# Attention and routed experts on one core: GpSimd's subtractions in four parts, and ScalarE in written order from step 117

## Chip, cores, metric

The kernel runs on one core of a Trainium2 chip. The metric is the device time of one launch in microseconds (us), lower is better. TensorE (PE) multiplies matrices, VectorE (DVE) and GpSimd (POOL) work elementwise, ScalarE (ACT) applies functions and copies, SyncE (SP) issues most of the DMAs. Each engine takes its instructions in the order in which they stand in its own queue, and waits for semaphores of the others.

## What is computed

Attention with rotary embedding over 4 batches, 8 heads, 576 positions and 64 dimensions, and behind it a mixture of 8 experts. A token takes the expert of its largest logit, or, where its local gate is at least one half, the expert of the token before it. Cut to what matters:

```python
scores = (rotate(q) @ rotate(k).T) / sqrt(64)
attn = softmax(scores)
x = (attn @ v) as rows of 512
logits = x @ w_gate; local = sigmoid(x @ w_local)
e[s] = argmax(logits[s]) if s == 0 or local[s] < 0.5 else e[s - 1]
p = softmax(logits[s])
out[s] = p[e] * (relu(x[s] @ w1[e]) @ w2[e])
```

## The kernel before

**Steps of the attention.** Two heads make a pair, so there are 16 pairs, and each has nine tiles of 128 queries: 144 steps g = 0 to 143 (line 1269 on). Step g does the following. DVE takes the minimum of the score tile (`mn`, line 278; the queries are negated). PE makes the scores of step g + 1 (`s`, line 273; two buffers of PSUM, so tile g + 1 needs the exponential of step g - 1 to have read its buffer). ACT takes the exponential (`e`, or `et` for the ninth tile; line 295). PE turns the tile of step g - 2 (`tm`, line 331, and `tk` or `tt` for what is left over), and PE multiplies by the values with a lag of eleven steps (`pv`, line 370).

**The high and low parts.** Matrices are multiplied as a high part and a rest. For a turned tile ACT casts the high part from PSUM (`pth`, line 309) and DVE subtracts it for the rest (`ptl`, line 313). For the steps' tiles in `ON_POOL` (125, 129, 130, 132, 134) `split_by_pool` is used in place of it: ACT copies the tile into SBUF (`stage`, line 304), GpSimd casts it (line 305) and GpSimd subtracts (line 306). The turned tiles, the products with v, the gate products `gx` and the routing's small products share four PSUM buffers. One is free again when its last reader is done.

**Gates and rows.** For a pair two places back, `gates` corrects the sums of the exponentials (ACT, lines 437 and 440; DVE's reciprocal, line 443), PE makes `gx` (line 456), and DVE or GpSimd scale it to logits `gm` (line 469) and to rows `xrow` (line 470), which go to DRAM.

**Routing.** When twelve pairs have their gates, at step 126, the routing of the first three batches is put into `todo`, one part of it for each step in the order of the string `ORDER`. It is a chain of small operations, mostly on DVE: maximum `mx`, difference `d`, exponential `ex` on ACT (line 531), code `c`, `f`, `key`, a scan over the tokens (line 564), the expert `e`, its one-hot `cnt` (line 581), a copy of it by ACT (`oha`, line 582), the running counts `cox`, the sum `se` (ACT adds 1e-9 on line 603), the product `d` with the one-hot on GpSimd (line 609), the probability `p` (lines 612 and 615), ranks (lines 632 to 647; fifteen compares on GpSimd on line 645) and the slots of the expert tiles (lines 682 to 709). Behind it GpSimd splits the first expert's weights (lines 894 and 895) and gathers rows (`x`, line 955). From step 143 on a written list (`DRAIN`) ends the attention. Then come the expert tiles: `tx` turns gathered rows (line 966), and the two products `h` and `o` follow (lines 980 and 1023).

**What sets the order.** Up to step 116 (`GM` is 117) every engine keeps the order in which the code is written. From step 117 to 143 the code runs under `tc.manual_schedule(engines=MAN0)`, and `MAN0` holds PE alone: a scheduler with due times of its own orders ACT, DVE, GpSimd and SP there. The scheduler can bring an operation forward as far as its inputs allow, also into the steps before 117. `late` is a list of work that each step runs behind its exponential.

```python
with tc.manual_schedule(engines=None if g < GM else MAN0):
    ...
    softmax_exp(g, mn)
    ...
    for f in late[:]:
        f()
        late.remove(f)
```

## Time and profile before

| | us |
|---|---|
| median of 3 runs | 538.23 (537.24 to 538.36) |
| profiled execution, its own time | 539.23 |
| profiled execution, span of its instructions | 537.5 |
| PE busy | 516.4 (96%) |
| DVE busy | 381.2 (71%) |
| ACT busy | 345.4 (64%) |
| POOL busy | 344.2 (64%) |

The profile is one execution. Busy shares are averages over stages with different limits: the steps of the attention up to about 285 us, then the expert tiles. Times in the rows below count from the first instruction. A figure in square brackets behind a row is the time for which that engine stood idle before it, and what ended the wait.

### The profile page before, as it was taken

Reading aid. Unit: us, or ns where it says so; the run is one execution under the profiler, and the core shown is the slowest. Engines: PE = TensorE matmul, PEld = TensorE weight load, DVE = VectorE, ACT = ScalarE, POOL = GpSimd, SP = SyncE. Lnnn points to the kernel's source line nnn. Section 1 sums busy time; section 2 is a strip of 40 time slices with the busy share of each in tenths; the row PEclk is TensorE's granted clock in tenths of the full one; section 3 lists DMA queues with packets and bytes.
Section 4 is the critical chain, followed back from the end, with each engine's and each line's share of the span. In section 5 each row is a group of like instructions: output and inputs, shape, how many; then the busy total and the mean of one; then the engine's idle time right before and its main releaser. Section 6 shows DMA issues by size and latency. Waiting matters only on the chain.

```text
span 537.5 us, 10798 instructions
## 1 busy us (share of the span) xinstructions
PE 516.4 (96%) x3273; PEld 459.1 (85%) x3273; DVE 381.2 (71%) x690; ACT 345.4 (64%) x766; POOL 344.2 (64%) x275
## 2 busy tenths in 40 slices
PE   7989999999999999999889999999999999999992
PEld 4889999999999999998889788887888888888881
DVE  6999999999999999999998746447421745421740
ACT  3988999999999999987667424352433344523440
POOL 4999999999999999694698202355512554411331
PEclk9999999999999999999999999999999999999998
DMA  8658788988889878865167214553537586637440
GB/s 277 277 133 223 223 221 230 239 187 213 222 224 241 213 188 217 239 157 134 21 221 212 70 29 168 183 211 107 187 101 234 142 331 167 187 99 234 107 150 25
DMA packets 65481, 97.33 MB, mean 181 GB/s; under 512 B 28353, under 2 KB 39105, under 8 KB 65282
## 3 DMA queue, kind: packets, MB, share of 16 engines
q1 hardware_dynamic: 61938, 86.45, 57.1%
q0 software_dynamic: 3040, 9.71, 5.8%
q8 instruction: 28, 0.46, 0.4%
q14 instruction: 43, 0.35, 0.2%
q10 hardware_dynamic: 432, 0.36, 0.2%
HBM read 76.95 MB, written 12.86 MB: 167 GB/s over the span
## 4 chain that ended last, share of the span: by engine, by line
PE 79%; DVE 10%; issue 3%; ACT 3%; POOL 2%; DMA 1%; ACTq 0%; POOLq 0%; DVEq 0%
PE h L980 18%; PE o L1023 17%; PE pv L370 14%; PE s L273 13%; PE tm L331 9%; PE gx L456 3%; DVE mn L278 3%; DVE ptl L313 2%; PE th L1014 2%; PE tx L966 1%; PE tk L341 1%; ACT e L295 1%; DVE w L925 1%; DMA turn<-in_turn_dram 1%; ACT w L922 1%
## 5 line engine op out<-in xcount | busy, mean ns | idle before, releaser
L1023 PE MATMUL o<-w,hs 128*128 128x512 f32 x456 | 113.0, 398 | 0.0
L278 DVE TENSOR_REDUCE mn<-s 128x1 f32<-128x576 f32 x144 | 107.1, 744 | 2.3 <-PE s L273 0.9
L295 ACT ACTIVATE e<-s,mn 128x576 f32<-128x576 f32 x128 | 95.5, 746 | 18.5 <-DVE mn L278 16.1
L980 PE MATMUL h<-w,xs 128*128 128x512 f32 x444 | 106.1, 392 | 0.8 <-DVE xs L313 0.5
L313 DVE TENSOR_TENSOR ptl<-tm,pth 128x512 fp32r<-128x512 f32 x139 | 95.5, 688 | 11.6 <-ACT pth L309 8.9
L1029 POOL DMA_INDIRECT out_dram<-os,sidx x19 | 23.2, 1223 | 124.1 <-ACTq L931 82.8
L273 PE MATMUL s<-m,qst 128*128 128x288 f32 x512 | 96.8, 311 | 4.7 <-ACT e L295 2.7
L980 PEld LDWEIGHTS h<-w,xs 128*128 128x128 f32 x444 | 82.6, 188 | 19.0 <-DVE w L925 1.1
L1023 PEld LDWEIGHTS o<-w,hs 128*128 128x128 f32 x456 | 83.1, 188 | 17.0 <-DVE hs L313 0.4
L309 ACT CAST pth<-tm 128x512 fp32r<-128x512 f32 x139 | 80.7, 581 | 6.8 <-PE tm L331 6.1
L273 PEld LDWEIGHTS s<-m,qst 128*128 128x128 f32 x512 | 74.0, 188 | 10.2 <-ACT e L295 5.4
L370 PE MATMUL pv<-pth,v 128*128 128x288 f32 x256 | 76.6, 314 | 0.5 <-DVE ex_row L723 0.4
L331 PE MATMUL tm<-wid,e 128*128 128x128 f32 x512 | 77.0, 272 | 0.0
L370 PE MATMUL pv<-ptl,v 128*128 128x288 f32 x256 | 76.3, 314 | 0.0
L200 POOL TENSOR_TENSOR stage<-stage 128x1152 f32<-128x1152 f32 x26 | 69.4, 2668 | 0.3 <-DMA stage<-in_qk_dram 0.3
L331 PEld LDWEIGHTS tm<-wid,e 128*128 128x128 f32 x512 | 62.0, 140 | 0.9 <-DVE ptl L313 0.3
L925 DVE TENSOR_TENSOR w<-stage,w 128x1024 fp32r<-128x1024 f32 x37 | 50.7, 1406 | 14.5 <-ACT w L922 9.4
L370 PEld LDWEIGHTS pv<-pth,v 128*128 128x128 f32 x256 | 48.3, 189 | 2.0 <-issue 0.6
L370 PEld LDWEIGHTS pv<-ptl,v 128*128 128x128 f32 x256 | 48.3, 189 | 0.0
L313 DVE TENSOR_TENSOR xs<-tx,xs 128x512 fp32r<-128x512 f32 x19 | 13.1, 689 | 44.3 <-ACTq L931 34.5
L201 POOL TENSOR_TENSOR stage<-stage 128x576 f32<-128x576 f32 x26 | 37.1, 1426 | 2.0
L313 DVE TENSOR_TENSOR hs<-th,hs 128x512 fp32r<-128x512 f32 x26 | 17.5, 688 | 27.9 <-ACTq L931 16.4
(202 smaller groups left out, 824.0 us busy)
## 6 DMA issues: line engine op xcount, KB each, us to landing
stage<-in_wts_dram SPq DMA_DIRECT2D x84, 512.0 KB
stage<-in_qk_dram SPq DMA_DIRECT2D x26, 576.0 KB
qst<-xq SPq DMA_DIRECT2D x56, 128.0 KB
stage<-in_v_dram SPq DMA_DIRECT2D x16, 320.0 KB
m<-xq SPq DMA_DIRECT2D x14, 288.0 KB
m<-xk SPq DMA_DIRECT2D x14, 288.0 KB
m<-xq SPq DMA_DIRECT2D x14, 256.0 KB
m<-xk SPq DMA_DIRECT2D x14, 256.0 KB
```

The source lines that it names most:

```text
L200: engine.tensor_tensor(x, x, tab[:, 2 * f:2 * f + 2], op=ALU.mult)
L201: engine.tensor_tensor(rr[:, f], x[:, 0], x[:, 1], op=ALU.add)
L273: pe.matmul(st[:, h, lo:hi], lhs, keys[:, k0:k0 + hi - lo], start=(n == 0), stop=(n == len(parts_) - 1))
L278: dve.tensor_reduce(mn, s_t[g][:, :, 0:HALF], axis=AX.XY, op=ALU.min)
L295: act.activation(dst.rearrange("p (h s) -> p h s", h=2), s_t.pop(g)[:, :, 0:HALF], AF.Exp, bias=mn, scale=-1.0, accum_out=sums[:, col:col ...
L309: act.copy(hi, src)
L313: dve.tensor_tensor(lo, src, hi.bitcast(F32), op=ALU.subtract)
L331: pe.transpose(ps[:, k], src[:, k * P:(k + 1) * P], ident)
L370: pe.matmul(pv_t[p, u], lhs.rearrange("p c d -> p (c d)"), rhs, start=(n == 0), stop=(n == 9))
L925: (pool if k in on_pool else dve).tensor_tensor(lo, src, hi.bitcast(F32), op=ALU.subtract)
L980: pe.matmul(ps[:, c], xs_t[t][:, x, k], w[y][:, c * 512:(c + 1) * 512], start=(k == 0 and n == 0), stop=(k == 3 and n == 2))
L1023: pe.matmul(ps, hs_t[t][:, x, k], w[y][:, (k % 2) * 512:(k % 2 + 1) * 512], start=(k == 0 and n == 0), stop=(k == 7 and n == 2))
```

## The change

There are two edits. `split_by_pool` subtracts in four instructions, one for each 128 columns, where there was one for all 512. `MAN0` takes in ACT, so that from step 117 ACT keeps the written order too; three operations of the first routing on ACT (`ex`, `oha` and the addition to `se`) are put into `late` and run behind the exponential of the next step. DVE, GpSimd and SP are still ordered by the scheduler there. Its answers differ where ACT's order differs.

```diff
-MAN0 = {PE_}
+MAN0 = {PE_, mybir.EngineType.Activation}
...
         pool.tensor_scalar(hi, x, 1.0, 1.0, op0=ALU.mult, op1=ALU.mult)
-        pool.tensor_tensor(lo, x, hi.bitcast(F32), op=ALU.subtract)
+        for k in range(4):
+            pool.tensor_tensor(lo[:, k], x[:, k], hi[:, k].bitcast(F32), op=ALU.subtract)
...
+        def on_act(f):
+            f() if final else late.append(f)
+
...
-            act.activation(ex, d, AF.Exp)
+            on_act(lambda: act.activation(ex, d, AF.Exp))
...
-            act.copy(oh, cnt[:, :, 1:n + 1].rearrange("p e j -> p j e"))
+            on_act(lambda: act.copy(oh, cnt[:, :, 1:n + 1].rearrange("p e j -> p j e")))
...
-            act.add(se, se, 1e-9)
+            on_act(lambda: act.add(se, se, 1e-9))
...
+        assert not late
```

Line numbers of the changed kernel are one higher from the new loop on, four higher from `route` on and five higher in the last part. In the rows below, the number behind a name's first underscore is its pair or a count, and for `tm`, `tk`, `s` and `mn` the step; the last number is a buffer's.

ScalarE from step 125 to step 127, before:

```order
L295 ACTIVATE e_13_3_4164,sum_3_3441<-s_125_4159,mn_125_4187 128x576
L440 ACTIVATE sum_3_3441<-sum_3_3441 128x10
L309 CAST pth_13_3994<-tm_123_4197 128x4x128
L309 CAST pth_13_3994<-tm_124_4216 128x4x128
L295 ACTIVATE et_14_4214,sum_3_3441<-s_126_4189,mn_126_4207 128x576
L531 ACTIVATE ex_5_4233<-d_4_4231 128x120
L295 ACTIVATE e_14_0_4251,sum_3_3441<-s_127_4209,mn_127_4244 128x576
```

The same place after:

```order
L295 ACTIVATE e_13_3_4164,sum_3_3441<-s_125_4159,mn_125_4187 128x576
L310 CAST pth_13_3994<-tm_123_4197 128x4x128
L295 ACTIVATE et_14_4214,sum_3_3441<-s_126_4189,mn_126_4207 128x576
L310 CAST pth_13_3994<-tm_124_4216 128x4x128
L295 ACTIVATE e_14_0_4250,sum_3_3441<-s_127_4209,mn_127_4243 128x576
L535 ACTIVATE ex_5_4233<-d_4_4231 128x120
```

The exponential of step 126 now stands ahead of the cast of tile 124, and the routing's `ex` behind the exponential of step 127. The addition to the sums is gone from here: those of three pairs, which the scheduler had brought forward, now stand at steps 121, 133 and 139.

ScalarE at steps 131 and 132, before:

```order
L304 COPY stage_94<-tm_129_4399 128x512
L295 ACTIVATE e_14_2_4397,sum_3_3441<-s_131_4365,mn_131_4390 128x576
L380 COPY tmp_13_4348<-pv_13_1_4378 64x288
L295 ACTIVATE e_14_2_4397,sum_3_3441<-s_132_4392,mn_132_4431 128x576
L582 CAST oha_107<-cnt_11_4422 128x120
```

The same place after:

```order
L295 ACTIVATE e_14_2_4400,sum_3_3441<-s_131_4368,mn_131_4393 128x576
L304 COPY stage_94<-tm_129_4402 128x512
L381 COPY tmp_13_4351<-pv_13_1_4381 64x288
L295 ACTIVATE e_14_2_4400,sum_3_3441<-s_132_4395,mn_132_4436 128x576
L586 CAST oha_107<-cnt_11_4428 128x120
```

The copy of tile 129, on which GpSimd waits, has gone behind the exponential of step 131.

VectorE around the minimum of step 124, before:

```order
L278 TENSOR_REDUCE mn_124_4157<-s_124_4122 128x1
L313 TENSOR_TENSOR ptl_13_3995<-tm_121_4128,pth_13_3994 128x4x128
L313 TENSOR_TENSOR pkl_13_3997<-tk_121_4135,pkh_13_3996 128x256
L469 TENSOR_TENSOR gm_2_3315<-gx_11_3_4146,sum_2_2278 128x2x18
L470 TENSOR_TENSOR xrow_11_3_4149<-gx_11_3_4146,sum_2_2278 128x256
L278 TENSOR_REDUCE mn_125_4187<-s_125_4159 128x1
```

The same place after:

```order
L314 TENSOR_TENSOR ptl_13_3995<-tm_121_4128,pth_13_3994 128x4x128
L314 TENSOR_TENSOR pkl_13_3997<-tk_121_4135,pkh_13_3996 128x256
L470 TENSOR_TENSOR gm_2_3315<-gx_11_3_4146,sum_2_2278 128x2x18
L471 TENSOR_TENSOR xrow_11_3_4149<-gx_11_3_4146,sum_2_2278 128x256
L278 TENSOR_REDUCE mn_124_4157<-s_124_4122 128x1
L278 TENSOR_REDUCE mn_125_4187<-s_125_4159 128x1
```

The minimum of step 124 has gone behind four operations. The minimum of step 142 goes behind the same four of tile 139 and `gx_13_3`.

## Rows read from the trace of the kernel before

**Rows 1.** The page's forty slices of the span, TensorE's busy share in tenths.

```profile
PE   7989999999999999999889999999999999999992
```

**Rows 2.** Busy time by engine in stretches of 10 us: stretch, length, busy (instructions) per engine.

```profile
260.00:270.00 10.00, 8.46 (x63) 7.72 (x63) 9.94 (x31) 6.95 (x18) 6.80 (x12) 1.00 0.24 32
270.00:280.00 10.00, 9.04 (x67) 8.13 (x66) 9.78 (x22) 6.61 (x16) 9.86 (x15) 1.00 0.73 250
```

**Rows 3.** Timeline of TensorE: start, duration, instruction, idle before and releaser.

```profile
244.62 0.80 PE L273 MATMUL s<-m,qst 128*128 128x288 f32 x4 [0.75 <-ACT et L295]
...
255.50 0.79 PE L273 MATMUL s<-m,qst 128*128 128x288 f32 x4 [0.64 <-ACT e L295]
...
261.87 1.01 PE L456 MATMUL gx<-wid,xt 128*128 128x146 f32 x6 [0.59 <-DVE ptl L313]
...
266.68 0.44 PE L341 MATMUL tk<-wid,e 128*128 128x128 f32 x2 [0.54 <-DVE ptl L313]
...
278.26 0.44 PE L341 MATMUL tk<-wid,e 128*128 128x128 f32 x2 [0.59 <-DVE ptl L313]
```

**Rows 4.** Timeline of VectorE, five operations of the routing.

```profile
255.36 1.70 DVE L581 TENSOR_TENSOR cnt<-cst,e 128x120 bf16<-128x120 f32 x1
...
259.02 1.20 DVE L615 TENSOR_TENSOR p<-p,se 128x15 f32<-128x15 f32 x1
...
264.23 0.99 DVE L647 SCALAR_TENSOR_TENSOR tcode<-e,lb 128x15 f32<-128x15 int32 x1
...
268.42 0.39 DVE L765 TENSOR_SCALAR wgt<-take 128x8 f32<-128x8 f32 x1
...
276.24 1.36 DVE L686 TENSOR_TENSOR ex<-c,cst 128x180 bf16<-128x180 bf16 x1
```

**Rows 5.** Timeline of GpSimd over the same time.

```profile
255.23 1.29 POOL L306 TENSOR_TENSOR ptl<-stage,pth 128x512 fp32r<-128x512 f32 x1
...
257.61 0.63 POOL L609 TENSOR_TENSOR d<-ex,oha 128x120 f32<-128x120 f32 x1 [1.10 <-ACT oha L582]
...
258.92 1.27 POOL L306 TENSOR_TENSOR ptl<-stage,pth 128x512 fp32r<-128x512 f32 x1
...
265.47 8.77 POOL L645 TENSOR_SCALAR ohr<-cst,lc 128x128 bf16<-128x128 bf16 x15
...
276.12 1.28 POOL L306 TENSOR_TENSOR ptl<-stage,pth 128x512 fp32r<-128x512 f32 x1
```

**Rows 6.** Two lines that run in both routings: shortest, median, longest in ns.

```profile
L581 DVE TENSOR_TENSOR cnt<-cst,e x2: 336/1019/1702, 255.4 to 312.9; 128x120 bf16<-128x120 f32 x1, 128x40 bf16<-128x40 f32 x1
...
L647 DVE SCALAR_TENSOR_TENSOR tcode<-e,lb x2: 156/575/994, 264.2 to 321.3; 128x15 f32<-128x15 int32 x1, 128x5 f32<-128x5 int32 x1
```

**Rows 7.** Timeline of GpSimd: a smaller operation on two inputs.

```profile
240.42 0.35 POOL L502 TENSOR_TENSOR gm<-gm 128x90 f32<-128x90 f32 x1
```

**Rows 8.** Timeline of VectorE around step 124.

```profile
237.91 0.75 DVE L278 TENSOR_REDUCE mn<-s 128x1 f32<-128x576 f32 x1
...
239.61 0.41 DVE L470 TENSOR_TENSOR xrow<-gx,sum 128x256 f32<-128x256 f32 x1
```

**Rows 9.** Timeline of ScalarE at steps 124, 126 and 131.

```profile
238.76 0.74 ACT L295 ACTIVATE e<-s,mn 128x576 f32<-128x576 f32 x1 [0.36 <-DVE mn L278]
...
243.24 0.59 ACT L309 CAST pth<-tm 128x512 fp32r<-128x512 f32 x1 [0.60 <-PE tm L331]
...
253.85 0.59 ACT L304 COPY stage<-tm 128x512 f32<-128x512 f32 x1 [1.42 <-PE tm L331]
```

**Rows 10.** Timeline where the attention ends: TensorE, GpSimd's first gather, TensorE.

```profile
285.76 0.98 PE L456 MATMUL gx<-wid,xt 128*128 128x146 f32 x6 [0.24 <-DVE ihi L700]
...
286.12 1.28 POOL L955 DMA_INDIRECT x<-rows_d,gidx  x1 [0.16 <-issue]
...
292.39 0.60 PE L966 MATMUL tx<-wid,x 128*128 128x128 f32 x4
```

**Rows 11.** The tile x between 285.5 and 287 us: the first gather's landing.

```profile
DMA to landing us min/median/max: 3.7/3.7/3.7
```

## The prediction

> **What bounds the kernel now.** I read the page's slices first: TensorE (PE) is at 9 tenths or more in nearly all of them, and the dip between 255 and 282 us is the one inside the span [rows 1]. That is steps 131 to 143, the routing of the first three batches beside the last attention tiles. By stretch, VectorE (DVE) is busy 9.94 and 9.78 of 10 us there while PE is busy 8.46 and 9.04, so PE stands idle 1.54 + 0.96 = 2.50 us in these 20 us [rows 2]. DVE sets the pace. PE's own waits name it: two are for an exponential (0.75 and 0.64 us), three for a subtraction of DVE's (0.59, 0.54 and 0.59 us) that frees a PSUM buffer [rows 3]. Before and behind this stretch PE is full, so a microsecond won here should arrive at the end, and one lost too.
>
> **Why DVE is slow there.** Four of its routing operations take 1.70, 1.20, 0.99 and 1.36 us [rows 4], far above their size. The line that takes 0.99 us with 15 elements takes 0.156 us with 5 in the other routing, and the one with 1.70 us for 120 elements takes 0.336 us for 40 [rows 6]. Three of the four end with a subtraction of GpSimd's: the probability runs from 259.02 to 260.22, and GpSimd's subtraction from 258.92 to 260.19; the operation from 276.24 ends at 277.60, 0.20 us behind GpSimd's 277.40; `cnt` ends 0.54 us behind 256.52, which is about its own time [rows 4, 5]. So a DVE operation of this kind stands until GpSimd's instruction is over. Minima and subtractions from PSUM beside them keep their usual time. During the fifteen compares of GpSimd, 8.77 us without a gap, a DVE operation of 8 elements takes 0.39 us [rows 4, 5]: it gets in between two of them.
>
> **The subtraction in four.** GpSimd's operation on 90 columns takes 0.35 us and on 512 columns 1.28 [rows 5, 7], a slope of 0.93 / 422 = 2.2 ns a column. A part of 128 is then 0.35 + 38 x 2.2 ns = 0.43 us (an estimate), four are 1.73, and each of the five subtractions costs GpSimd 0.45 us more. The upper bound is a compare of 128 columns, 8.77 / 15 = 0.58, so 2.34 and 1.06 us more; the lower is no cost at all, 1.28. I take 0.45, the row of the same operation. A DVE operation caught behind it now waits at most 0.43 us (0.58), on average half of that, in place of up to 1.28.
>
> The rows show only DVE standing. The Trainium skill, "SBUF — State Buffer", section "Who interferes with whom", says that the port pair which the two share is an exclusive lock for a whole instruction, and that the one that issues second blocks, whichever it is. By that, DVE can now also get in front of three more parts and hold up GpSimd; no row here shows GpSimd held. Each such case would cost GpSimd a DVE operation of about 0.2 us, and the sum below would come out 0.2 us worse.
>
> **The four blocked operations, one by one.** (a) `cnt` at step 132 and (b) the probability at step 133: their excess is 1.16 and about 1.03 us. But ACT's written order takes much of it back. The copy of tile 129 ran at 253.85, in an idle stretch of ACT's, ahead of the exponential of step 131 [rows 9]. Now it stands behind that exponential, whose buffer PE waits for until 255.50 [rows 3], so it starts at about 255.45, 1.6 us later. GpSimd then casts until 256.8 and subtracts until 258.55, and the product `d` that stands behind it starts at 258.6 where it started at 257.61 [rows 5]. It ends at 259.2. DVE, in order, has finished `cnt` early (255.9, since GpSimd is idle) and all behind it by 257.5, and then stands until 259.2 for `d`. The probability runs into the next cast of GpSimd and ends near 260.1, against 260.22. Gain here: 0.1, so I write 0. With parts of 0.58 us it is a loss of 0.5.
>
> (c) The line with 0.99 us at 264.23: it now waits 0.2 us for a part and takes about 0.16. Against it stand ACT's correction of the sums of pair 12 (now at step 133, 0.4 us before the copy of tile 132) and DVE's reciprocal of 0.13, both moved here from where PE was full. DVE is then 0.3 us earlier (between 0 and 0.5), and of PE's 0.54 us at 266.68 [rows 3] 0.3 go. (d) The line with 1.36 us at 276.24 becomes 0.3 to 0.7: only one part of tile 134's subtraction stands ahead of GpSimd's next work. The subtraction behind it comes 0.7 us or more earlier, and the whole 0.59 us at 278.26 [rows 3] goes. I take 0.59.
>
> **ACT's written order at step 126.** Before, the exponential of step 126 stood behind a cast for which ACT idled 0.60 us at 243.24 [rows 9], and PE waited 0.75 us for it at 244.62 [rows 3]. It now stands ahead. The new times in this paragraph are estimates: every operation keeps its duration and starts when its inputs and its engine are there. The scheduler has answered on DVE: the minimum of step 124, at 237.91 before, stands behind the row product, which ended at 239.61 + 0.41 = 240.02 [rows 8]. Without the minimum in front, these products end at 239.55. The minimum then runs to 240.2, and the exponential of step 124 starts at 240.2 instead of 238.76 [rows 9]. PE needs its buffer for the scores of step 126, and those of step 127 need the next exponential: PE is 0.45 us late there, then 0.83 (scores of 127 at 242.8). Behind the next minimum (242.65 to 243.35) the exponential of step 126 runs from 243.5 to 244.15, and PE's five products with v are over at 244.6. So PE is at 244.6 in both: the 0.75 us wait is gone, and as much has been spent ahead of it. Sum: 0 (between -0.7 and +0.8). Up to step 130 ACT and DVE then stand as before.
>
> **The end of the stretch.** The minimum of step 142 goes behind four operations in the same way. By its inputs, exponential 142 starts at about 280.4 and the one of step 143 at 282.1, 0.4 us earlier than now, although PE is 0.9 earlier. PE's wait at 285.76 for DVE [rows 10] grows from 0.24 to about 0.5. Given back: 0.3 us.
>
> **GpSimd's chain and its cover.** From the cast of tile 132 to the first gather GpSimd has no gap. The two subtractions inside add 0.9 us and the later start 0.2, so the gather goes from 286.12 to 287.2 and lands 3.7 us behind that [rows 10, 11], at 290.9. PE needs it at 292.39 [rows 10], or 291.8 after a gain of 0.6. The cover is 0.9 us. With parts of 0.58 us the gather is 1.2 us later still, and the missing 0.3 us would be paid in full. SP's queue keeps its order; the loads that wait for GpSimd's weight splits come a microsecond later and are for the second expert tile.
>
> **Sum.** 0 (step 126) + 0 (a, b) + 0.3 (c) + 0.59 (d) - 0.3 (end) = 0.6 us less. Against the profiled execution's own 539.23 that is 538.6; this execution is 1.0 above the median of the runs, 538.23, and from that it is **537.6**. A measurement of this kernel can tell about 0.2% from no change, that is 1.08 us, so the forecast is "the same".
>
> **Rivals.** *DVE's time arrives whole.* If the parts are cheap, or `d` doesn't hold DVE, then four operations lose 4.1 us of excess less a part each (4 x 0.43), 2.4 us, and PE's idle 2.50 us in the stretch [rows 2] fall to about 0.4. That is 2.1 less: 536.1. For it: DVE is the engine that is full. Against: ACT puts GpSimd later just where two of the four are. *The minima late.* The exponentials of steps 124 and 142 stand behind row products, and PE doesn't recover what it loses: 0.83 at step 127, 0.7 at the end, 0.5 at step 133 for `d`, against 0.9 won at (c) and (d). That is 1.1 more: 539.4. It decides from the point at which exponential 126 ends behind 244.4. For it: DVE and ACT had no slack at 238 to 244 beyond what I counted, 0.36 us before exponential 124 [rows 9]. Against: the exponential of step 126 no longer waits for a cast. *The port isn't given up between parts.* Then DVE stands 1.7 us instead of 1.28, (c) and (d) are gone, and the result is 0.3 more: 538.5. Against it are the fifteen compares [rows 4, 5], between which DVE did get in.
>
> **How the numbers follow.** Forecast 0.42, DVE's time whole 0.30, minima late 0.18, port kept 0.10. Below 537.15 lie the second and a small part of the first: faster 0.36. Above 539.3 lies the third: slower 0.18. The rest, 0.46, is the same. The forecast's own range is 537.0 to 538.5. To leave out 2 in 10, the range runs from a little below 536.1 to a little above 539.4.
>
> **What would show it.** Right: the line of `cnt` at 0.5 us and that of 276.24 below 0.8; DVE idle 1 us or more before the sum of `p`, waiting for GpSimd's `d`; no wait of PE at the scores of step 128; idle time of ACT for the minimum of step 124 above 1 us; the wait for a subtraction at tile 139's `tk` gone; the first gather near 287. Wrong: PE's idle time between 260 and 280 below 1 us (the second case), or above 3 us (the third); four parts in more than 2.1 us; a wait of PE at the first `tx`.

## The result, and the profile after

The changed kernel takes 541.96 us (median of 6 runs, 541.10 to 544.24) against 538.22 (6 runs): a ratio of **1.0074, 95% interval 1.0056 to 1.0091**. It is slower, by 3.7 us. The forecast was 537.6, the range ended a little above 539.4, and the case "slower" had 0.18. The profiled execution has a span of 539.6 us and takes 541.53.

The stretches of 10 us, as in [rows 2] (length, then busy time and instructions of PE, PEld, DVE, ACT, POOL, granted clock, DMA):

```profile
240.00:250.00 10.00, 8.12 (x61) 7.51 (x60) 9.55 (x19) 8.23 (x22) 4.86 (x7) 1.00 0.60 142
250.00:260.00 10.00, 9.29 (x73) 8.37 (x72) 8.30 (x17) 7.62 (x20) 5.27 (x12) 1.00 0.32 73
260.00:270.00 10.00, 9.37 (x72) 8.83 (x71) 9.84 (x35) 7.63 (x20) 8.04 (x17) 1.00 0.26 32
270.00:280.00 10.00, 8.51 (x63) 7.59 (x61) 9.82 (x22) 6.86 (x17) 9.86 (x18) 1.00 0.67 211
280.00:290.00 10.00, 8.94 (x80) 8.27 (x79) 7.99 (x23) 6.69 (x16) 9.37 (x9) 1.00 0.82 246
290.00:300.00 10.00, 8.84 (x55) 7.89 (x54) 8.13 (x14) 7.16 (x12) 7.58 (x6) 1.00 0.57 150
```

The three of them in which the difference lies, before:

```profile
240.00:250.00 10.00, 9.14 (x69) 8.48 (x69) 9.00 (x23) 8.57 (x22) 6.34 (x10) 1.00 0.58 145
...
280.00:290.00 10.00, 9.73 (x87) 8.99 (x86) 8.64 (x25) 7.24 (x16) 9.06 (x7) 1.00 0.91 241
290.00:300.00 10.00, 9.96 (x59) 8.67 (x58) 9.43 (x17) 7.30 (x12) 7.27 (x6) 1.00 0.48 124
```

PE is idle 0.63 + 1.49 = 2.12 us between 260 and 280, near the 2.50 of before. New are 1.88 us between 240 and 250 (0.86 before), 1.06 in 280 to 290 (0.27) and 1.16 in 290 to 300 (0.04). So the loss is on either side of the stretch that the prediction worked on. PE's waits, as in [rows 3]:

```profile
240.88 1.03 PE L273 MATMUL s<-xq,qtail 128*128 128x288 f32 x6 [0.74 <-POOL lg_all L505]
...
245.39 0.80 PE L273 MATMUL s<-m,qst 128*128 128x288 f32 x4 [0.90 <-ACT et L295]
...
277.90 0.44 PE L342 MATMUL tk<-wid,e 128*128 128x128 f32 x2 [1.21 <-DVE ptl L314]
...
285.07 0.66 PE L332 MATMUL tm<-wid,e 128*128 128x128 f32 x4 [0.74 <-DVE ptl L314]
...
294.17 0.63 PE L970 MATMUL tx<-wid,x 128*128 128x128 f32 x4 [1.16 <-DMA x<-rows_d,gidx]
```

The wait for ScalarE's exponential at 244.62 is still there (0.90 us at 245.39) where it was to vanish; one of 0.74 is added ahead of it, before the scores of step 126. The profile infers `lg_all` as what ended that one, but `lg_all` was done at 240.49; these scores need the buffer that exponential 124 had read at 240.69, just before they start. The wait at tile 139's `tk`, which was to vanish, went from 0.59 to 1.21 in this execution. And the first `tx` of the experts waits 1.16 us for the first gather's data; it didn't wait before [rows 10].

VectorE, as in [rows 4], with the routing's `d` and `c8` (printed `c`) in front. The first line is `c8` before:

```profile
245.33 0.27 DVE L536 SCALAR_TENSOR_TENSOR c<-d,cst 128x120 f32<-128x120 f32 x1
```

```profile
240.79 0.52 DVE L532 TENSOR_TENSOR d<-lg_all,mx 128x120 f32<-128x120 f32 x1
241.34 1.50 DVE L540 SCALAR_TENSOR_TENSOR c<-d,cst 128x120 f32<-128x120 f32 x1
...
256.06 0.67 DVE L585 TENSOR_TENSOR cnt<-cst,e 128x120 bf16<-128x120 f32 x1
...
259.84 0.28 DVE L616 TENSOR_REDUCE p<-d 128x15 f32<-128x120 f32 x1 [1.49 <-POOL d L613]
260.15 0.26 DVE L619 TENSOR_TENSOR p<-p,se 128x15 f32<-128x15 f32 x1
...
264.31 0.32 DVE L651 SCALAR_TENSOR_TENSOR tcode<-e,lb 128x15 f32<-128x15 int32 x1
...
275.43 1.81 DVE L690 TENSOR_TENSOR ex<-c,cst 128x180 bf16<-128x180 bf16 x1
```

Three of the four long operations are short, as forecast: `cnt` 0.67 (1.70), the probability 0.26 (1.20), `tcode` 0.32 (0.99), and 1.49 us of idle time for GpSimd's `d` stand ahead of the sum of `p`. But the operation on `ex` took 1.81 us (1.36), and `c8`, which took 0.27 before, took 1.50. GpSimd beside them, as in [rows 5] and [rows 10]:

```profile
241.27 1.44 POOL L213 TENSOR_TENSOR xq<-stage,xq 128x576 fp32r<-128x576 f32 x1
...
250.41 1.71 POOL L307 TENSOR_TENSOR ptl<-stage,pth 128x128 fp32r<-128x128 f32 x4
...
275.75 0.62 POOL L305 TENSOR_SCALAR pth<-stage 128x512 fp32r<-128x512 f32 x1
276.34 0.72 POOL L218 TENSOR_SCALAR v<-stage 128x640 fp32r<-128x640 f32 x1
277.14 0.25 POOL L770 TENSOR_SCALAR after<-take 128x8 f32<-128x8 f32 x1
...
277.65 0.45 POOL L307 TENSOR_TENSOR ptl<-stage,pth 128x128 fp32r<-128x128 f32 x1
...
279.57 1.28 POOL L307 TENSOR_TENSOR ptl<-stage,pth 128x128 fp32r<-128x128 f32 x3
...
288.00 1.28 POOL L959 DMA_INDIRECT x<-rows_d,gidx  x1 [0.16 <-DVE ipad L711]
```

`c8` ended 0.13 us behind GpSimd's split of `xq` (242.71). A subtraction in four took 1.71 us, against 1.73 estimated. `ex` began beside the last compare, stood through two casts and ended at 277.24, 0.18 us behind the second cast's end (277.06), where GpSimd leaves a gap of 0.08. ScalarE, as in [rows 9]:

```profile
239.95 0.74 ACT L295 ACTIVATE e<-s,mn 128x576 f32<-128x576 f32 x1 [1.92 <-DVE mn L278]
...
281.22 0.74 ACT L295 ACTIVATE e<-s,mn 128x576 f32<-128x576 f32 x1 [2.46 <-DVE mn L278]
```

ScalarE idles 1.92 and 2.46 us ahead of the two exponentials behind a late minimum, 124 and 142.

Executions differ by up to 1 us before the changed part begins. So the table counts from the start of exponential 123, the last place that the kernels reach alike: all columns but the first are starts in the profiled execution's timelines, less that start. "Tile 2" is the first product of the second token tile that reads the lower part of `xs` (the tile's rows, turned, as a high and a lower part), "end" the end of the last product.

| kernel | exp 123 at | exp 126 | exp 141 | exp 143 | compares | 1st gather | 1st `tx` (wait) | tile 2 | end | ratio, 95% |
|---|---|---|---|---|---|---|---|---|---|---|
| before | 236.51 | 7.21 | 40.23 | 46.00 | 28.96 | 49.61 | 55.88 (0) | 67.21 | 290.63 | 1 |
| changed | 236.13 | 8.38 | 39.54 | 46.85 | 30.43 | 51.87 | 58.04 (1.16) | 69.37 | 293.73 | 1.0074 (1.0056 to 1.0091) |
| changed, more products behind 300 us | 236.52 | 8.36 | 39.66 | 45.81 | 30.40 | 51.61 | 57.24 (1.40) | 70.30 | 293.80 | 1.0046 (1.0030 to 1.0061) |
| parts alone | 235.82 | 7.23 | 38.68 | 44.02 | 26.96 | 48.94 | 55.93 (1.87) | 67.25 | 290.77 | 0.9986 (0.9975 to 0.9997) |
| order alone | 235.93 | 8.35 | 40.48 | 47.45 | 29.65 | 50.66 | 57.33 (0) | 68.67 | 292.18 | 1.0057 (1.0036 to 1.0078) |
| changed, tile 134 whole | 236.27 | 8.36 | 39.64 | 45.78 | 30.39 | 51.16 | 56.83 (1.01) | 68.81 | 292.29 | 1.0037 (1.0023 to 1.0051) |
| changed, minimum 142 ahead | 236.37 | 8.36 | 39.64 | 44.94 | 30.38 | 51.60 | 57.15 (1.85) | 70.32 | 295.36 | 1.0069 (1.0046 to 1.0093) |
| changed, minimum 124 ahead | 235.56 | 5.88 | 36.70 | 42.84 | 27.45 | 48.67 | 54.63 (1.75) | 67.36 | 290.87 | 1.0025 (1.0006 to 1.0044) |
| changed, both ahead | 236.22 | 5.88 | 36.68 | 41.99 | 27.43 | 48.65 | 54.16 (1.80) | 67.37 | 290.81 | 1.0007 (0.9993 to 1.0020) |

So the changed kernel loses 1.17 us at step 126, wins 1.86 back up to step 141, loses 1.54 up to step 143, and 1.31 more up to the first `tx`. Its last product ends 3.1 us later. The medians differ by 3.7; the three of its six runs with a mean granted clock of 0.995 or 0.996 (541.10, 541.53, 542.39) have a median 3.3 above that of before. The rest is the clock, further down.

**What one execution shows and others don't.** Three of the experiments below (the store later, the gathers first, more products) run the changed kernel's instructions in its order on all engines up to step 143. In their traces `ex` took 0.76, 0.33 and 0.77 us in place of 1.81, PE has no wait at tile 139's `tk`, and exponential 143 is at 45.77, 45.34 and 45.81 in place of 46.85. `d` and `c8` are the same in all four (0.51 to 0.53 and 1.48 to 1.50), and so is step 126 (8.35 to 8.38). `ex` with the two casts of GpSimd, in the one with more products:

```profile
275.82 0.77 DVE L690 TENSOR_TENSOR ex<-c,cst 128x180 bf16<-128x180 bf16 x1
...
275.67 0.73 POOL L305 TENSOR_SCALAR pth<-stage 128x512 fp32r<-128x512 f32 x1
276.37 0.80 POOL L218 TENSOR_SCALAR v<-stage 128x640 fp32r<-128x640 f32 x1
```

Here it got in behind the first cast. The long stand isn't a single freak either: with both minima ahead `ex` took 0.76 us, and 1.81 with the store later besides. So the loss at step 126 belongs to the changed order, and the 1.81 us, with the wait at `tk` and 1 us of the loss up to step 143, to the profiled execution. Without them step 143 isn't later than before, and PE still reaches the first `tx` 1.4 us late (57.24).

### The profile page after: what moved, and what is told of

The parts are those of the page before. It is cut to its first block, busy times and chain, and to the rows that moved or that the text cites. A ratio compares the mean times of both kernels' runs of the same rounds, so it can differ in the third digit from the quotient of the medians.

```text
span 539.6 us, 10816 instructions
## 1 busy us (share of the span) xinstructions
PE 516.1 (96%) x3273; PEld 458.7 (85%) x3273; DVE 379.8 (70%) x690; ACT 344.7 (64%) x766; POOL 346.7 (64%) x290
```

## The experiments

My theory after the traces, ORDER: the new order costs the time, by the minima behind the row products and by `d` and `c8` beside GpSimd's split. Its rival, PARTS: GpSimd's longer chain makes the first gather late.

### Each half alone

The parts alone (kernel before, all other engines' order unchanged):

```
-        pool.tensor_tensor(lo, x, hi.bitcast(F32), op=ALU.subtract)
+        for k in range(4):
+            pool.tensor_tensor(lo[:, k], x[:, k], hi[:, k].bitcast(F32), op=ALU.subtract)
```

> The kernel before with one edit: GpSimd's five subtractions run in four instructions each; the order on TensorE, VectorE, ScalarE and SyncE is that of before. Theory ORDER (the 4 us that the change costs come from the new order: VectorE takes the minima of steps 124 and 142 behind row products, and `d` and `c8` of the routing meet GpSimd's split of xq at 241): nothing of that is here, the routing operations of 1.70, 0.99 and 1.36 us shrink below 0.8, and the time is 536.2 to 537.6 (ratio 0.996 to 0.999). Theory PARTS (the four instructions lengthen GpSimd's chain, and its first gather comes behind TensorE's need): the first gather starts at 287 or later, TensorE waits at the first tx, and the time is 538.8 to 540 (ratio 1.001 to 1.003).

Measured: 537.34 us, 0.9986 (0.9975 to 0.9997). The blocked operations, on VectorE:

```profile
254.68 0.85 DVE L582 TENSOR_TENSOR cnt<-cst,e 128x120 bf16<-128x120 f32 x1
...
257.58 0.18 DVE L616 TENSOR_TENSOR p<-p,se 128x15 f32<-128x15 f32 x1
...
262.06 0.17 DVE L648 SCALAR_TENSOR_TENSOR tcode<-e,lb 128x15 f32<-128x15 int32 x1
...
271.97 1.83 DVE L683 TENSOR_TENSOR c<-code,tcode 128x90 bf16<-128x90 f32 x1
...
274.39 0.55 DVE L687 TENSOR_TENSOR ex<-c,cst 128x180 bf16<-128x180 bf16 x1
```

`cnt` 0.85, `p` 0.18, `tcode` 0.17 and `ex` 0.55 for 1.70, 1.20, 0.99 and 1.36: 3.5 us less. The operation from `code` (printed `c`) grew from 0.23 at 275.42 to 1.83. The attention's last exponential comes 1.98 us earlier than before, about the 2.1 that the rival "DVE's time arrives whole" gave. But at the first `tx` nothing of it is left in this execution, and the medians give 0.7: the first gather, 0.67 us earlier, landed 6.9 us behind its start instead of 3.7 [rows 11], and PE waits 1.87 us.

```profile
DMA to landing us min/median/max: 6.9/6.9/6.9
...
291.75 0.63 PE L967 MATMUL tx<-wid,x 128*128 128x128 f32 x4 [1.87 <-DMA x<-rows_d,gidx]
```

The time is in ORDER's range, though PARTS' wait at `tx` is there too. The order alone is the reverse of that edit on the changed kernel.

> The changed kernel with GpSimd's subtractions whole again: the order alone. Theory ORDER: the exponentials of steps 124 and 142 start as late as in the changed kernel (239.9 and 281.2), the blocked routing operations are long again (1 to 1.7 us), so what the parts won is lost too: 541.5 to 543 (ratio 1.006 to 1.009). Theory PARTS: GpSimd's chain is 2.2 us shorter over the five tiles, the first gather starts near 286, no wait at the first tx: 538 to 539.5 (ratio 1.000 to 1.002).

Measured: 540.73 us, 1.0057 (1.0036 to 1.0078). That is between the two ranges, nearer to ORDER's: 2.7 us by the medians are there without any part. By the trace it costs 1.55 us at the end (290.63 to 292.18), half of the changed kernel's 3.1; three of the six runs, at a clock of 0.994 to 0.996, took 538.91 to 540.41, and three, at 0.991 and 0.992, 541.05 to 543.03. In detail the forecast was half a miss: there is no wait at `tx` (the gather landed in 3.5 us), and `cnt` and `p` are short here too (0.67 and 0.26), so the order alone shortens these two, as the parts alone do. `ex` is 1.35.

### Tile 134 whole

```
-    def split_by_pool(hi, lo, src):
+    def split_by_pool(hi, lo, src, n=4):
...
+        for k in range(0, 4, 4 // n):     # n = 1 for tile 134
...
```

> The changed kernel, but GpSimd's subtraction for tile 134, the last of the five, in one instruction. Theory ORDER: minima and routing stand as in the changed kernel, the time is 541.3 to 542.6 (ratio 1.006 to 1.008). Theory PARTS, in the form that the last three parts of tile 134, run at 279.57 to 280.85 behind the split of v, hold back the weight loads and with them the first gather: the weight loads start 2 to 3 us earlier, the gather is at 286 to 287 in place of 288.0, the wait of 1.16 us at the first tx goes, and the time is 540.3 to 541 (ratio 1.004 to 1.005).

Measured: 539.88 us, 1.0037 (1.0023 to 1.0051): 2 us better than with all five in parts. PARTS holds for this one tile: its last three parts stood behind the split of v, and SyncE's weight loads, which go into the same buffer, waited for them. The waits of SyncE's queue between 260 and 285 us (waiting line, releaser, total us, times, longest), of the changed kernel and then of this one:

```profile
SPq L881 <- POOL ptl L307: 8.1, 1, 8.1
```

```profile
SPq L883 <- POOL ptl L308: 5.7, 1, 5.7
```

The gather starts 0.71 us earlier (0.45 against the execution with more products, whose wait was 7.2), the last product ends 1.4 us earlier. The wait at `tx`, which was to go by PARTS, is still 1.01.

### The minima

Both minima ahead; then each alone with `(141,)` or `(123,)`:

```
-                if g < GM - 1:
+                if g < GM - 1 or g in (123, 141):
                     minima[g + 1] = softmax_min(g + 1)
```

> The changed kernel, but the minima of steps 124 and 142 are written a step ahead, so that VectorE takes each ahead of the subtraction and the row products, as in the kernel before; the operations `d` and `c8` move back too, the orders of TensorE and ScalarE stay as in the changed kernel. Theory ORDER: exponential 124 starts at about 238.8 and 142 near 279, the gain of 1.1 us that the changed kernel has by step 141 stays and the 0.8 lost at step 126 is not lost: 537 to 538.8 (ratio 0.998 to 1.001), and most of the wait at the first tx goes as the row store and the weight splits come earlier. Theory PARTS: the gather remains at 287.5 or later with a wait at the first tx, 540.5 to 542 (ratio 1.004 to 1.007).

Measured: 538.87 us, 1.0007 (0.9993 to 1.0020). ORDER holds: 3.1 us of the median come back, `c8` takes 0.28 us, and the last exponential comes 4.86 us earlier than in the changed kernel's profile (3.82 than with more products) and 4.01 earlier than before. The wait at `tx` stays, as PARTS had it.

> The changed kernel with the minimum of step 142 alone a step ahead; the minimum of step 124 and the operations `d` and `c8` stay where the change has them. Theory BOTH (each of the two late minima costs what its place shows: 0.8 us at 126, 2.1 us at 142): exponential 142 at 279.3 or earlier, exponentials up to 141 as in the changed kernel, 539.5 to 541 (ratio 1.003 to 1.0055), between the changed kernel and the one with both moved. Theory 142 (nearly all the loss is the last one, as it stands next to the end of the attention and steps 126 to 135 have slack): 538.2 to 539.2 (ratio 1.0005 to 1.002). Theory 124: no less than 541.2.

Measured: 542.66 us, 1.0069 (1.0046 to 1.0093): no gain, as theory 124 has it. The last exponential did come 1.91 us earlier (0.87 than with more products), but the gather only 0.27 (0.01), and PE waited longer for it (1.85 us). Its profile also shows the lower clock (0.66 in 305 to 310), but the three runs at 0.994 to 0.996 have the median of the changed kernel's three, 541.53. So the end of the attention isn't what sets the time in the changed kernel. That GpSimd's chain behind it does is argued from the table; the gather's start alone doesn't, as the run with the gathers first shows further down.

> The changed kernel with the minimum of step 124 alone a step ahead; with it VectorE's `d` and `c8` move back behind the next subtraction and minimum, and the minimum of step 142 stays late. The complement of the run with 142 alone, which won nothing (542.66). Theory 124 (what the change loses is lost at steps 124 to 126, and arrives because GpSimd's fifteen compares, its weight splits and the first gather all come later by it): exponential 126 near 242.1, the compares at 263.7 in place of 266.6, the first gather near 285, and 538.3 to 539.5 (ratio 1.000 to 1.002), as with both minima moved. Theory BOTH NEEDED: 540.3 or more (ratio 1.0035 or more).

Measured: 539.15 us, 1.0025 (1.0006 to 1.0044). The minimum of step 124 (with `d` and `c8`, which the scheduler moves back with it) carries the loss. Exponential 126 comes 2.50 us earlier than in the changed kernel, the compares 2.98, the gather 3.20, the end 2.86. No run tells apart which of the two costs more, the minimum or `c8`, as both moved. The changed kernel's trace allows an estimate. `d` and `c8` took 2.02 us where they took 0.54 before, and from them VectorE goes over two more operations to the minimum of step 126, at 243.73, without a gap above 0.03 us, though the scores for it are there at 241.91. Without these 1.48 us exponential 126 would start at 6.9, ahead of the 7.21 of before. By that, `d` and `c8` beside GpSimd's split are what loses the time at step 126, and the late minimum by itself loses none there.

### Why the attention's gain doesn't arrive

With both minima ahead the attention ends 4.0 us earlier than before, and the last product 0.2 later. Two things take it: the gather's landing, and VectorE's subtractions for the weights, which come 1.7 us earlier by the table's count and then stand beside GpSimd's. VectorE and GpSimd with both minima ahead:

```profile
293.61 5.40 DVE L929 TENSOR_TENSOR w<-stage,w 128x1024 fp32r<-128x1024 f32 x3
...
293.25 2.41 POOL L929 TENSOR_TENSOR w<-stage,w 128x1024 fp32r<-128x1024 f32 x1
```

and before, where GpSimd's 2.4 us lay beside operations of VectorE that read PSUM:

```profile
295.59 3.53 DVE L925 TENSOR_TENSOR w<-stage,w 128x1024 fp32r<-128x1024 f32 x3
...
293.38 2.39 POOL L925 TENSOR_TENSOR w<-stage,w 128x1024 fp32r<-128x1024 f32 x1
```

**The landing.** In the kernels that keep the gathers' place it went with the store of pair 14's first rows (192 KB): 3.5 to 3.7 us where the store was issued 2.07 us or more behind the gather's start (before, order alone, and two of those below), 5.4 to 7.3 where it was 0.67 to 0.71 behind. The store was moved behind pair 14's last one; TensorE's and ScalarE's order changes a little behind 320 us.

```
-            if engine is pool:
+            if engine is pool or p == NPAIR - 2:
                 stores.append(lambda: store(j0, n, xr))
```

> The changed kernel, but the store of the first three row blocks of pair 14 (192 KB, issued at 288.68, 0.7 us behind the first gather's start) goes behind pair 14's last store, that is behind two weight loads, at about 296; TensorE's and ScalarE's order changes a little behind 320 us. Theory COLLISION (the gather's packets stand behind that store in the DMA engines: landing took 3.5 and 3.7 us where the store was issued 2.1 to 2.4 us behind the gather's start, and 5.4 to 6.9 where it was issued 0.67 to 0.7 behind): the landing falls to 3.5 to 4 us, the wait of 1.16 us at the first tx goes, and the time is 540.5 to 541.2 (ratio 1.0045 to 1.006). Theory LOADS (the weight loads of 512 KB alone make the landing long): landing stays above 5, the time stays 541.5 to 542.5 (ratio 1.0065 to 1.0085).

Measured: 543.14 us, 1.0092 (1.0069 to 1.0115). In the trace COLLISION holds: the gather starts at 51.59 as in the changed kernel (51.87), and `tx` at 55.65 without a wait, 2.4 us earlier (1.6 than with more products). In the time it is a miss: the kernel got slower. The page has the reason: TensorE's granted clock, at nine tenths or more in all slices but the last of the changed kernel's profile, is down in one. By stretches of 5 us:

```profile
295.00:300.00 5.00, 5.00 (x25) 3.98 (x23) 5.00 (x3) 3.66 (x5) 4.73 (x4) 1.00 0.84 189
300.00:305.00 5.00, 2.49 (x13) 1.79 (x12) 4.85 (x10) 2.42 (x5) 2.58 (x2) 0.84 0.36 105
305.00:310.00 5.00, 4.48 (x13) 2.73 (x13) 3.82 (x6) 0.00 (x0) 0.00 (x0) 0.50 0.01 3
```

PE was busy 2.49 of 5 us in 300 to 305; there it waited 1.84 us for the second token tile's `xs`, because it was early and ScalarE and VectorE were not. In 305 to 310 the clock is 0.50, the lower of its two levels (1.2 GHz).

> The changed kernel with the minima of 124 and 142 a step ahead (1.0007 by itself, first tx at 290.4 with a wait of 1.80 us) and with the store of pair 14's first three row blocks behind pair 14's last store. Theory COLLISION: the landing of the first gather falls from 5.4 to below 4, the wait at tx from 1.8 to 0.3, the next gathers land earlier too, and the time is 536 to 537.5 (ratio 0.996 to 0.9985). Theory LOADS: nothing of that, 538 to 539.3 (ratio 0.9995 to 1.002). A third outcome: tx comes earlier and the time stays, because the two waits for `xs` at 301 and 303 (0.99 and 1.00 us) grow by as much; then the bound is the second token tile.

Measured: 539.46 us, 1.0008 (0.9991 to 1.0025): the third outcome. `tx` at 52.96 without a wait, the waits for `xs` 1.82 and 1.00 us, tile 2 at 67.37 as with the wait, the clock 0.79 in 305 to 310.

> Three edits on the changed kernel: the minima of 124 and 142 a step ahead, tile 134's subtraction in one instruction, the store of pair 14's first row blocks behind pair 14's last store. Theory COLLISION, with the weight loads freed by tile 134's subtraction 2 to 3 us earlier: first gather near 284, landing below 4, no wait at the first tx, 535 to 536.8 (ratio 0.9945 to 0.998), faster than the kernel before and than the one with four parts alone. Against it (the operation that was blocked at 276 is blocked again, 1.36 us in place of 0.5, and the store is no cause): 537.5 to 538.5 (ratio 0.999 to 1.001).

Measured: 539.75 us, 1.0013 (0.9994 to 1.0032), a miss. Tile 2 is the earliest of all so far (66.65), and the clock falls to 0.65 between 300 and 305: two runs at a mean clock of 0.994 and 0.995 took 536.8 and 537.2, the nine at 0.988 to 0.990 took 538.7 to 540.9.

**The gathers first**, ahead of the split of the weight block w_q:

```
-ORDER = ".....fs.rRe.klx.c0pt...wg.1.Gi"
+ORDER = ".....fs.rRe.klx.c0pt...wg.G.1i"
```

> The changed kernel, but GpSimd issues its four gathers ahead of the split of the second weight block (w_q, 3.5 us) instead of behind it. Every other engine keeps its order. Theory GATHER (behind the attention the end is set by GpSimd's chain to the first gather and its landing): the gather starts near 286.0, when VectorE has its indices, instead of 288.0, lands before TensorE needs it at 293.0, the wait of 1.16 us at the first tx goes, and the time is 540.4 to 541.3 (ratio 1.0045 to 1.006). Theory WEIGHTS (the next thing in line is as late: w_q, the weight loads behind it and VectorE's subtractions for the weights, which then stand beside GpSimd's): tx comes earlier, and the first product of the second token tile not: 541.5 to 542.5 (ratio 1.0065 to 1.0085).

Measured: 541.91 us, 1.0070 (1.0043 to 1.0097): WEIGHTS. The gather starts at 48.55, 3.3 us earlier, and its data come 8.2 us behind that, in the middle of the weight loads; PE still waits 1.35 us, and tile 2 is at 69.48. Here the store was 2.4 us behind, so the store is one cause of a long landing and not the only one. The two runs at a clock of 0.995 and 0.996 took 540.75 and 540.40, inside GATHER's range, so the clock may hide a part of what it wins; two runs don't show it.

> The kernel before with the subtraction in four (0.9986 by itself; attention 2.7 us earlier, of which 0.7 arrive, and a wait of 1.87 us at the first tx) and with the four gathers ahead of the split of w_q. Theory GATHER: the first gather starts near 283 instead of 284.76, lands by 290 even if landing still takes 6.9 us, tx at 290 instead of 291.75, and the time is 535.6 to 536.8 (ratio 0.995 to 0.9978). Theory WEIGHTS: the second token tile's products stay where they are (303.07), with longer waits ahead of them and perhaps a lower granted clock behind these: 537 to 539 (ratio 0.998 to 1.0015).

Measured: 541.67 us, 1.0055 (1.0040 to 1.0070). `tx` at 53.91 without a wait, as GATHER says, tile 2 at 67.88, as WEIGHTS says, and the clock down again, in every run (0.988 or 0.989); the time is above both ranges. By stretches:

```profile
300.00:305.00 5.00, 2.68 (x7) 1.34 (x8) 4.68 (x11) 1.69 (x4) 0.35 (x1) 0.78 0.29 93
305.00:310.00 5.00, 5.00 (x15) 3.91 (x14) 1.50 (x2) 0.00 (x0) 0.00 (x0) 0.53 0.00 0
```

**GpSimd's weight subtractions in four**, the change's own idea one stage later, here for the blocks `w`; `w_m` and `w_q` have the same loop:

```
...
+                n = 4 if t == 0 and k in on_pool else 1
+                for i in range(n):
+                    s = slice(i * 1024 // n, (i + 1) * 1024 // n)     # tensor_tensor on [:, s]
```

> The changed kernel with the minima of 124 and 142 a step ahead, and with GpSimd's subtractions for the weights of the first token tile (1024 columns, 2.4 us each: w_m, w_q and one more) in four instructions of 256 columns. Without the second edit VectorE's three weight subtractions from 293.6 took 5.40 us (3.53 in the kernel before, where GpSimd's 2.4 us lay beside operations that read PSUM). Theory PORT (VectorE's subtraction with both inputs in SBUF stands until GpSimd's instruction is over): the three take 3.5 to 4.3 us, the operation of 1.85 us at 282.9 falls below 0.8, and the third group of products of the second token tile starts at 302.5 or earlier in place of 303.59: 537 to 538.3 (ratio 0.998 to 1.0005). Theory WEIGHTS LATE (they stood for the weight loads, not for GpSimd): three still above 5 us, 538.5 to 539.3 (ratio 1.0005 to 1.002).

Measured: 539.54 us, 1.0024 (1.0009 to 1.0039). VectorE's three take 4.63 us in place of 5.40, and the operation of 1.85 us takes 0.60, so PORT holds in kind, though not in time. GpSimd pays: its own takes 3.84 in place of 2.41 (2.8 in four pieces where VectorE doesn't subtract weights beside it), the gather starts 1 us later, and `tx` waits 2.90.

> The kernel before with the subtraction in four, the gathers ahead of the split of w_q, and GpSimd's weight subtractions for the first token tile in four; no change of order on TensorE, VectorE, ScalarE and SyncE. If GATHER and PORT both hold, the first tx is at 290 or earlier, the second token tile's third group at 301.5 to 302.3, and more than half of the 2.7 us that the attention wins reaches the end: 535 to 536.5 (ratio 0.9945 to 0.997), faster than before and than the four parts alone. If the end of the attention and the experts are bound by something else (the weight loads, the second gather's landing), 536.8 to 538 (ratio 0.9975 to 1.0).

Measured: 539.84 us, 1.0015 (0.9996 to 1.0034), a miss. Here the two engines alternate, and GpSimd stands:

```profile
293.41 5.39 DVE L931 TENSOR_TENSOR w<-stage,w 128x1024 fp32r<-128x1024 f32 x3
...
294.45 5.62 POOL L931 TENSOR_TENSOR w<-stage,w 128x256 fp32r<-128x256 f32 x4
```

The clock is down in this profile too (0.65 and 0.67 in the two stretches from 300 to 310); the five runs at 0.994 and 0.995 took 537.4 to 538.5, the six at 0.988 to 0.992 took 539.8 to 541.7.

### The clock

Six more products of 512 columns on TensorE, in the rest ahead of the second token tile, first on the kernel with the parts and the gathers first:

```
+        if t == 1:
+            old = xs_t[0][:, 0]
+            for n in range(6):
+                pe.matmul(ps[:, n % 2], old[:, 0], old.rearrange("p k n -> p (k n)"), start=True, stop=True)
         for k in range(4):
             w = w_t.pop((t, k))
```

> The kernel with the subtraction in four and the gathers first (1.0055; the first tx earliest of its kind at 289.8 with no wait, and the time 3 us worse than before, the granted clock 0.78 and 0.53 at 300 to 310) with six more products of 512 columns on TensorE ahead of the first product of the second token tile, where it waited 1.50 us; their result is overwritten. Theory CLOCK (TensorE's rests between 295 and 304 are followed by a stretch at the lower granted clock, which costs 3 us): the clock stays near 1.00 at 300 to 310, and the time is 537.3 to 538.7 (ratio 0.9975 to 1.000). Theory OTHER (the time is lost in the experts' own waits, the clock goes with it by chance): 541 to 543 as without the products.

Measured: 539.02 us, 1.0011 (0.9995 to 1.0027), against 1.0055 without the products. CLOCK holds, 0.3 us above its range. The same stretches:

```profile
300.00:305.00 5.00, 3.72 (x16) 2.08 (x15) 4.72 (x9) 1.68 (x4) 0.14 (x1) 1.00 0.28 84
305.00:310.00 5.00, 5.00 (x26) 4.08 (x26) 1.55 (x3) 1.10 (x2) 0.00 (x0) 1.00 0.00 0
```

Tile 2 starts at the same time in both (303.77 and 303.58); from there to the last product's end it is 226.36 us without them and 223.47 with them. The stretch at the lower level cost 2.9 us.

> The changed kernel with the same six products on TensorE ahead of the first product of the second token tile. In runs of the changed kernel with a mean granted clock of 0.989 to 0.992 the time was 541.5 to 544.2, with 0.995 to 0.996 541.1 to 542.4. Theory CLOCK: the runs near 0.99 vanish, the median goes to 541.0 to 541.8 and the spread shrinks below 1.5 us; what is left, 3 us, is the late gather's and the attention's. If the products themselves stand in the way (the wait there was short, 0.78 us further on), 542 to 543.5.

Measured: 541.35 us, 1.0046 (1.0030 to 1.0061), no run below a clock of 0.993. The six runs of the changed kernel had 0.995, 0.995 and 0.996 (541.10, 542.39, 541.53), 0.992 (541.46), and 0.990 and 0.989 (543.43, 544.24). So its clock costs 0.6 us by the medians, 1.5 by the ratios; 2.5 us, 0.46%, are left without it. The spread hardly shrinks (2.7 us, 3.1 without the products), where I had expected less than 1.5.

> The changed kernel with the minima of 124 and 142 a step ahead, tile 134's subtraction whole, the store of pair 14's first row blocks later (1.0013 with these three: 536.8 and 537.2 in its two runs at a clock near 0.995, 538.7 to 540.9 in the nine near 0.99) and with the six products ahead of the second token tile. Theory CLOCK: all runs are like the first two, 536.3 to 537.5 (ratio 0.996 to 0.998): faster than the kernel before and no slower than the four parts alone (0.9986). Theory OTHER: 539 to 540.5 as without the products.

Measured: 538.30 us, 0.9989 (0.9975 to 1.0004): CLOCK again (1.0013 without the products), though above the range that I gave. In its profile VectorE's three subtractions also miss GpSimd's (3.53 us, against 6.54 without the products), so part of this gain may be that; why they miss is open. Up to step 143 both run the same order on VectorE, and here too executions differ: `ex` 1.35 against 0.77, the last exponential at 44.34 against 42.01.

> The kernel before with the subtraction in four (0.9986, all its runs at a clock of 0.993 to 0.996) and the six products on TensorE ahead of the second token tile. Theory CLOCK: there was no drop to take away here, the products fit in the wait or cost up to 0.8 us: 537 to 538.5 (ratio 0.998 to 1.0005). If these products help by something else than the clock, it gets faster here too: below 536.8 (ratio below 0.9975).

Measured: 538.33 us, 0.9994 (0.9979 to 1.0010): no gain where no clock was lost. So, as far as this shows, the products act by the clock.

> The kernel before, its order kept on all engines up to the end of the attention, with the subtraction in four for the first four tiles and whole for tile 134, the store of pair 14's first row blocks behind pair 14's last one, and the six products ahead of the second token tile. By the runs so far: the attention 2 to 2.7 us earlier, the weight loads not held back by tile 134's last parts, the gather's landing near 4 us, no drop of the clock: 535.5 to 537 (ratio 0.995 to 0.998), the fastest of all. Against it: the third group of products of the second token tile stays at 303 as in most kernels here, 537.3 to 538.5 (ratio 0.9985 to 1.0005).

Measured: 538.40 us, 1.0001 (0.9988 to 1.0014), a miss; it is in the range that I gave as the case against. With tile 134 whole, the operation on `ex` stands 1.35 us again, against 0.55 with parts, in the same order:

```profile
275.11 1.35 DVE L689 TENSOR_TENSOR ex<-c,cst 128x180 bf16<-128x180 bf16 x1
```

PE waits 1.57 us at tile 139's `tk`, and the last exponential is at 46.15, behind that of before. So tile 134 in parts is worth its 0.8 us on VectorE in before's order, where `ex` stands beside that subtraction. In the changed order `ex` comes ahead of it (0.77 with tile 134 whole, too), and the parts only delay the weight loads.

The parts alone are the best kernel found, 0.9986, with an interval that ends just below 1; the changed order with three repairs and the products (0.9989) isn't distinguishable from it. What bounds most of these kernels is behind the attention: tile 2 lies between 67.2 and 67.9 in before and in eight other versions, whose last exponential is anywhere from 42.0 to 46.0; what is won ahead goes to the landing or to VectorE's wait beside GpSimd's weight subtraction. That these two are all of it is not shown.

## Why the prediction was wrong, point by point

**What bounds the kernel** was read rightly for 255 to 282 us, and too narrowly: that a microsecond won there "should arrive at the end" holds for PE's own queue, but behind the attention PE needs the first gather, and that hangs on GpSimd's chain. With the parts alone 1.98 us won become 0.7.

**The parts**: right in size (1.71 us; 1.73 forecast). The sentence that each DVE operation then "waits at most 0.43 us" was wrong: `c` took 1.83 us with the parts alone, and `ex` 1.81 in the profiled execution, each through several GpSimd instructions.

**(a), (b)**: right. `cnt` is short, the copy of tile 129 is late (256.11 in place of 253.85), and DVE stands 1.49 us for `d`. The step is confirmed by the order alone, where both are short without any part.

**(c)**: too small, and credited to the wrong half. Between exponentials 135 (263.02 before, 263.79 now) and 136 (265.99, 265.40) the changed kernel wins 1.36 us where 0.3 stood in the sum, but the order alone shows the same distance (263.12 to 264.73). What the parts win there comes later, at the operation from `code`: 0.31 us against 1.44 with the order alone.

**(d)**: right in its result in three of four traces, wrong in the profiled one. "Only one part of tile 134's subtraction stands ahead of GpSimd's next work" overlooked that by its own steps the operation comes earlier, and so beside the last compare and two casts that follow each other without a gap. In the profiled execution it stood through both casts, and in place of 0.59 won, 0.62 were lost at `tk`. In the three others it took 0.33 to 0.77, and the wait at `tk` is gone, as forecast. That it got in there is luck as far as these runs tell. With the parts alone `ex` took 0.55, but the 1.83 of `c` ahead of it left a wait of 0.76 at `tk`.

**Step 126**: wrong, and the decisive one; this is the step that failed. I forecast exponential 126 from 243.5 to 244.15 and gave an end behind 244.4 as the point from which the rival "minima late" decides; it starts at 244.51. Missing in the paragraph are `d` and `c8`, which the same reordering sets ahead of the subtraction and so beside GpSimd's split of `xq`: 0.52 and 1.50 us in place of 0.27 each. The paragraph's own working was near: it put exponential 126 at 7.0 by the table's count, and 6.9 is what the estimate further up leaves without the stand of these two. The term of 0 (-0.7 to +0.8) measured +1.17 (1.14 to 1.17 in all seven traces with that order at step 126), and it goes on downstream: compares 1.47 us later. With minimum, `d` and `c8` moved back, 1.0074 becomes 1.0025.

**The end**: 0.3 given back; the profiled execution gave back 1.54, from 0.69 ahead at step 141 to 0.85 behind at step 143, but 1 us of it comes with `ex`. In the traces with the store later and with more products it is 0.4, with the gathers first nothing. And this term cost nothing: minimum 142 ahead didn't change the time.

**GpSimd's chain and its cover**: wrong in both ends. The gather came 2.26 us later, not 1.1: the compares start 1.47 us later and last 9.21 us (8.77), and the parts behind them add 0.45. With the store later and with more products it came 2.0 later, with the compares at 8.78 in the first of these. And the landing is no constant: with the row store 0.68 us behind the gather, not 2.07, the data came about 6 us behind its start, not 3.7. A cover of 0.9 us became a wait of 1.16.

**The rivals**: "minima late" named the place and put 539.4 on it; it left out `d` and `c8`, the gather and the clock. It deserved more than 0.18: its point of decision lay 0.25 us behind the forecast's own time, a sum of several estimates. "DVE's time whole" is what the parts do up to the last exponential when the order stays (1.98 us of 2.1); at the end 0.7 are left. "The port isn't given up between parts" fell in the main: with the parts alone `cnt` takes 0.85 us and `tcode` 0.17 beside them. But `c` began beside the last part and didn't get in behind it (1.83).

**The page** of the Trainium skill that the prediction weighed ("SBUF — State Buffer", section "Who interferes with whom") says that whichever engine issues second blocks. No row of before showed GpSimd held; these runs do (2.41 us whole, and 2.8 in four pieces, become 3.84 and 5.62 in four pieces beside VectorE's weight subtractions), so the trace agrees.

## What to carry to other kernels

Cutting a GpSimd instruction doesn't free VectorE by itself: look at what GpSimd runs next, and at which operation will stand there after the reordering, not before. What stands there may get in or not from one execution to the next (`ex`, 0.33 to 1.81 us), so read such a row in more than one trace before you give it a cause. A gain counts from the point where the next stage needs it: follow each engine's chain (here routing, compares, weight splits, gather, landing) to that point and compare the slack of each, because the stage that comes early meets transfers and operations which it used to miss. And where one engine gets faster and its partner doesn't, the rest that opens on TensorE may cost clock as well as time; cheap products in the rest show it, and take it away.

## What the runs showed of the hardware

- A VectorE operation with both inputs in SBUF can stand through several GpSimd instructions in a row: `c` 1.83 us with the parts alone, `ex` 1.81 in the profile of the change, where the longest single one was 0.73. The same `ex`, in the same order of instructions on all engines, took 0.76, 0.33 and 0.77 in three other executions, and got in there behind a cast or a compare that the next GpSimd instruction follows without a gap. What decides is open.
- GpSimd is held too: with VectorE's 1.2 us subtractions beside it, its work of 2.4 us took 3.84 and 5.62 in four pieces, 2.8 in four pieces without them.
- The gather of 128 rows landed 3.5 to 3.7 us behind its start or 5.4 to 7.3 (8.2 by PE's wait, with the gathers first), by what else was in the DMA engines: moving one store took the wait at `tx` away.
- TensorE's granted clock fell to its lower level between 300 and 310 us where PE had just rested for the second token tile: busy 2.49 us of the 5 from 300 on with the store later, 2.68 with the parts and the gathers first. A rest alone doesn't tell: with both minima ahead PE was busy 2.89 there and kept the full clock in its profile, with minimum 142 ahead 3.25, and the clock was 0.66 in 305 to 310. The price by rows was 2.9 us, near the 3.1 that the changed kernel's trace lost at a full clock.
